# Cutting the last 24 units of a fused attention and MLP kernel into three chunks, two of them with the output's tokens on partitions in a new order

## The chip, the core and the metric

The kernel runs on one core of a Trainium2 chip. The metric is the device time of one execution in microseconds: the median of three runs, 104.57 us for the kernel before (103.97 to 104.58). The profile is of one further execution, which took 104.39 us.

A core has a matrix engine (PE, with its weight loads shown apart as PEld), a vector engine (DVE), an activation engine (ACT), a general engine (POOL) and a queue processor (SP). Here SP issues nearly all DMA transfers. ACT issues a few. Matmuls write into PSUM, from where DVE or ACT carry results to SBUF, and DMA transfers carry them to memory.

## What is computed

A linear attention with a product feature map, for 4 batches, 4 heads, 1088 positions and 32 values per head, and then an MLP over all 4352 tokens:

```python
def phi(x):                       # 8 x 8 = 64 features
    a = np.einsum('rd,bhsd->bhsr', S1, x)
    b = np.einsum('rd,bhsd->bhsr', S2, x)
    return np.einsum('bhsi,bhsj->bhsij', a, b).reshape(*x.shape[:-1], r * r)
q_p, k_p = (phi(q), phi(k))
kv = np.einsum('bhsf,bhsd->bhfd', k_p, v)
z = np.sum(k_p, axis=2)
num = np.einsum('bhsf,bhfd->bhsd', q_p, kv)
den = np.einsum('bhsf,bhf->bhs', q_p, z)[..., None] + 1e-06
attn = num / den
x = attn.transpose(0, 2, 1, 3).reshape(4352, 128)
h = x @ w_in                      # 128 -> 2048
g = h * (1.0 / (1.0 + np.exp(-beta * h)))
out = g @ w_out                   # 2048 -> 128
```

## The kernel before, in words

**Tokens and units.** The 1088 positions of a batch are read as 32 tokens by 34 units: position s is token s // 34, unit s % 34. `xall` (128 x 4352, 2-byte) holds x for all batches, features on partitions and one column per token. Within a batch its columns run unit by unit, 32 tokens each, so column `b * 1088 + u * 32 + t`.

**Attention.** For each batch, steps named by a short code and the batch number make the features, sums and quotients. The last of them is `num`, which writes the batch's x into four strips of PSUM, one for each unit modulo 4: two banks of the tile `xp` and two of `xw`, which takes its place from the same pair of buffers as the MLP's waves. Three copies then bring the strips to `xall`: `xb` (strip 3), `xa` (strip 2), both from `xw`, and `xc` (strips 0 and 1, from `xp`). For the last batch `xb3` runs on ACT, `xa3` and `xc3` on DVE (the function `x_copy`, L579 to L591).

**MLP.** The 136 units of all batches are cut into chunks: eight of 16 units (512 tokens) and a last one of 8 units (256 tokens). A chunk is worked through in waves. A wave fills a PSUM tile of 1024 columns with h for some of the 16 blocks of 128 hidden values (two blocks for 512 tokens, four for 256). This first product is the steps `f<wave>a` and `f<wave>b` (L705, one half of the tile each), with w_in already multiplied by beta, followed by one Silu on ACT into `gT` (L716). The second product, `s<wave>a` and `s<wave>b`, adds that wave's share to the chunk's accumulator (L737): w_out is the weight operand and `gT` streams, so that the result has the 128 output features on partitions and tokens along the row. There are 68 waves: f0 to f63 for the eight large chunks, f64 to f67 for the last.

**Stores.** `o<chunk>` (the function `store`) turns 32 x 32 blocks of a finished accumulator with one DVE transposition into `osb` (L664), and stores it with four transfers per batch that it touches (L670), each for 32 output features: rows of 128 B, 32 tokens as the outermost dimension. The last chunk is different (`store_last`). Its second product has `gT` as the weight operand and w_out streaming (L729), so tokens come out on partitions, two blocks of 128 of them in the two banks of one tile `fin`. Partition p of a block is unit p // 32, token p % 32. ACT copies one bank, DVE the other (L685), and each is stored by one transfer of 128 rows of 512 B, from ACT's queue and from SP's (L686), with the 4 units as the outermost dimension and the 32 tokens inside.

**Order.** Nothing is scheduled automatically. The string `ORDER` lists all steps, and each engine carries out its part in that order. The end of it is: the copies of the last batch around f46 and f47, then chunks 6, 7 and 8, whose second products run some waves behind the first, with o5 and o6 in between, o7 between f67a and f67b, and o8 last.

**PSUM tiles.** `wave` has two buffers. `att2` (two banks: `kpp`, `qpp`, `xp`, at the end `fin`), `acc` (the accumulator of the large chunks) and `att1` (one bank: the small sums of a batch) have one each.

Of the kernel before, what the change touches and what calls it, by code (L numbers as in the profile page):

```python
# [7 lines left out]
F32 = mybir.dt.float32  # L8
F16 = mybir.dt.float16
ALU = mybir.AluOpType  # L10
ACTF = mybir.ActivationFunctionType

P = 128
T = 32
# [3 lines left out]
def kernel(  # L18
# [12 lines left out]
    nc = tc.nc  # L31

    B, H, S, D = q.shape
    R = S1.shape[0]
    F = R * R
    NTOK, DM = out.shape
    DFF = moe_w_in.shape[1]
    NJ = DFF // P
    U = S // T
# [32 lines left out]
    f47a f47b s40b s41a s41b f48a f48b s42a s42b f49a f49b s43a s43b f50a f50b s44a s44b s45a f51a f51b s45b  # L72
    s46a f52a f52b s46b s47a s47b f53a f53b f54a o5 f54b s48a s48b s49a f55a f55b s49b s50a f56a f56b s50b s51a
    f57a f57b s51b s52a s52b f58a f58b s53a s53b f59a f59b s54a s54b s55a s55b f60a f60b f61a o6 f61b s56a s56b
    s57a s57b f62a f62b s58a s58b f63a f63b s59a s59b s60a f64a f64b s60b s61a f65a f65b s61b s62a s62b f66a
    f66b s63a s63b f67a o7 f67b s64a s64b s65a s65b s66a s66b s67a s67b o8
    """

    ENGINES = {
# [12 lines left out]
    ps = ctx.enter_context(tc.tile_pool(name="ps", bufs=1, space=bass.MemoryType.PSUM))  # L92
    ctx.enter_context(tc.manual_schedule())

    def ap(t, offset, dims, p0=0, pn=None):
        pd = list(t.ap[0])
        s = t if pn is None else t[p0 : p0 + pn]
        return bass.AP(tensor=s.tensor, offset=s.offset + offset, ap=[list(s.ap[0])] + dims)

    def ct(shape, dtype, name):  # L100
        return const.tile(shape, dtype, tag=name, name=name)
# [33 lines left out]
    xall = ct([P, B * S], F16, "xall")  # L135

    wave_t = lambda n: ps.tile([P, 2, 512], F32, tag="wave", bufs=2, name=n)
    att2_t = lambda n: ps.tile([P, 2, 512], F32, tag="att2", name=n)
    acc_t = lambda n: ps.tile([P, 512], F32, tag="acc", name=n)

    st = [dict() for _ in range(B)]
# [178 lines left out]
    def eng(name):  # L320
        return {"v": vec, "p": pool}[ENGINES[name]]
# [239 lines left out]
    def num(b, c0, c1):  # L561
# [4 lines left out]
        for f in range(2):  # L566
            for h in range(H):
                for j in range(4):
# [7 lines left out]
                        stop=(f == 1),  # L576
                    )

    def x_copy(b, j, c0, c1, eng):  # L579

        n = min(c1, (U - max(j, 0) + 3) // 4) - c0
        if j < 0:
            eng(
                out=ap(xall, b * S + c0 * P, [[T, 2], [P, n], [1, T]]),
                in_=ap(st[b]["xp", c0][0], 0, [[512, 2], [T, n], [1, T]]),
            )
        else:
            eng(  # L588
                out=ap(xall, b * S + c0 * P + j * T, [[P, n], [1, T]]),
                in_=ap(st[b]["xp", c0][j], 0, [[T, n], [1, T]]),  # L590
            )  # L591


    KC = ((0, 2), (2, 4), (4, 6), (6, 9))
    XPARTS = (("x", (0, 4)), ("", (4, NC)))
    for b in range(B):
# [36 lines left out]
        for x, (c0, c1) in (("", (0, NC)),) if b else XPARTS:  # L633
            step(f"num{x}{b}", num, b, c0, c1)
            for n, j in (("xa", 2), ("xb", 3), ("xc", -1)):
                step(
                    f"{n}{x}{b}",
                    lambda b=b, j=j, c0=c0, c1=c1, k=f"{n}{x}{b}": x_copy(b, j, c0, c1, cop(k)),
                )


    chunks = []
    u = 0
    for n in (16,) * 8 + (8,):
        chunks.append((u, n))
        u += n
    assert u == B * U and chunks[-1][1] == 8
    waves = []
    for ci, (u0, un) in enumerate(chunks):
        per = 1024 // (un * T)  # L650
# [2 lines left out]

    gts, accs, wvs = {}, {}, {}

    LAST = len(chunks) - 1

    def store(ci):
        u0, un = chunks[ci]
        if ci == LAST:  # L660
            store_last(u0, un)
            return
        osb = sb.tile([P, 16, T], F32, tag="osb", bufs=3, name="osb")
        nc.vector.transpose(out=osb[:, :un, :].rearrange("p u m -> p (u m)"), in_=accs[ci][:, : un * T])  # L664
        done = 0
        while done < un:
            b, u = divmod(u0 + done, U)
            n = min(un - done, U - u)
            for m in range(4):
                nc.sync.dma_start(  # L670
                    out=bass.AP(
                        tensor=out.tensor,
                        offset=out.offset + (b * S + u) * DM + m * T,
                        ap=[[U * DM, T], [DM, n], [1, T]],
                    ),
                    in_=osb[T * m : T * m + T, done : done + n, :],
                )
            done += n

    def store_last(u0, un):  # L680

        b, u = divmod(u0, U)
        for i, (copy, e) in enumerate(((nc.scalar.copy, nc.scalar), (nc.vector.tensor_copy, nc.sync))):
            o = ct([P, DM], F32, f"fin_sb{i}")
            copy(out=o, in_=accs[LAST][:, i, 0:DM])  # L685
            e.dma_start(  # L686
                out=bass.AP(
                    tensor=out.tensor,
                    offset=out.offset + (b * S + u + 4 * i) * DM,
                    ap=[[DM, 4], [U * DM, T], [1, DM]],  # L690
                ),
                in_=o,
            )

    def first(s, w):
        ci, n, per, j0 = waves[s]
        u0, un = chunks[ci]
        if s % GP == 0 and w == 0:
            gts[s // GP] = sb.tile([P, GP * 1024], F16, tag="gT", bufs=GB, name="gT")
        if w == 0:  # L700
            wvs[s] = wave_t("wave")
        half, g, o = per // 2, gts[s // GP], s % GP * 1024
        for i in range(half):
            j = j0 + w * half + i
            nc.tensor.matmul(  # L705
                out=wvs[s][:, w, i * n : i * n + n],
                lhsT=winb[:, j * P : j * P + P],
                rhs=xall[:, u0 * T : u0 * T + n],
                start=True,
                stop=True,  # L710
            )
        if s == len(waves) - 1 and w:
            for i in range(2):
                nc.scalar.activation(out=g[:, o + 512 * i : o + 512 * i + 512], in_=wvs[s][:, i], func=ACTF.Silu)
        elif w:
            nc.scalar.activation(  # L716
                out=g[:, o : o + 1024], in_=wvs[s].rearrange("p a n -> p (a n)"), func=ACTF.Silu
            )

    def second(s, w):  # L720
        ci, n, per, j0 = waves[s]
        if j0 == 0 and w == 0:
            accs[ci] = att2_t("fin") if ci == LAST else acc_t("acc")
        half = per // 2
        for i in range(half):
            j, o = j0 + w * half + i, s % GP * 1024 + w * 512 + i * n
            if ci == LAST:
                for a in range(2):
                    nc.tensor.matmul(  # L729
                        out=accs[ci][:, a, 0:DM],  # L730
                        lhsT=gts[s // GP][:, o + a * P : o + a * P + P],
                        rhs=woutp[:, j, :],
                        start=(j == 0),
                        stop=(j == NJ - 1),
                    )
                continue
            nc.tensor.matmul(  # L737
                out=accs[ci][:, :n],
                lhsT=woutp[:, j, :],
                rhs=gts[s // GP][:, o : o + n],  # L740
                start=(j == 0),
                stop=(j == NJ - 1),
            )

    for s in range(len(waves)):
        for w in range(2):
            step(f"f{s}{'ab'[w]}", first, s, w)
            step(f"s{s}{'ab'[w]}", second, s, w)
    for ci in range(len(chunks)):
        step(f"o{ci}", store, ci)  # L750
# [37 lines left out]
```

## Time and profile before

| | |
|---|---|
| median of the runs | 104.57 us (103.97 to 104.58) |
| the profiled execution | 104.39 us |
| its span | 102.6 us, granted clock 0.998 |
| PE busy | 95.2 us (93%), 1294 matmuls |
| ACT busy | 72.3 us (70%) |
| DVE busy | 59.1 us (58%) |
| DMA queue q1 (SP's) | 24756 packets, 12.29 MB, 44.6% of 16 engines |
| chain that ended last | PE 86%, ACT 7%, DVE 1% |
| Silu of 128x1024, L716 | 67 times, mean 1024 ns |
| first product, 128x512 and 128x256, L705 | 144 times, 40.7 us busy |
| second product, 128x512, L737 | 128 times, 36.9 us busy |
| turned second product, 128x128, L729 | 32 times, 1.9 us busy |

The span runs from the first to the last instruction of the program that the profiler saw, so it is shorter than the time of the execution by what lies around it, here 1.8 us. The time column of a matmul counts from its issue to the end of its flow through the array. Matmuls overlap, so the distance between two starts is what one costs in a row of them: 0.43 us for two of 512 columns in the chain. A queue's packets are the pieces that the 16 DMA engines moved, a few bytes of signalling included.

The lines that answer to the places which the change touches stand in the prediction.

### The profile page before, as it was taken

How to read it: one execution, taken by the hardware profiler on the slowest of the kernel's cores; microseconds unless marked ns; L12 is line 12 of the kernel's file. 1: busy time of each engine (PE TensorE's matmuls, PEld its weight loads, DVE VectorE, ACT ScalarE, POOL GpSimd, SP SyncE). 2: the span in 40 equal slices, each digit the busy share in tenths (PEclk: the TensorE clock that was granted, in tenths of full speed). 3: DMA queues.
4: the chain of work that ended last, by engine and by line, in shares of the span. 5: the costliest groups of instructions: out<-in, count | busy, mean ns of one | idle time of the engine just before them, and what ended most of it. 6: DMA issues, size and time to landing. Idle time of an engine off the chain costs nothing.

```text
span 102.6 us, 3065 instructions
## 1 busy us (share of the span) xinstructions
PE 95.2 (93%) x1294; PEld 45.0 (44%) x1294; DVE 59.1 (58%) x107; ACT 72.3 (70%) x92; POOL 40.7 (40%) x49
## 2 busy tenths in 40 slices
PE   5999989999999999999999999999999999999900
PEld 1234554344445454345446433644534444446800
DVE  1564888999798995898953967489240020200210
ACT  1412022687695984789995879999979999899710
POOL 6409689989997993008090000094000000000000
PEclk9999999999999999999999999999999999999999
DMA  2999999986661446613320261051004132022250
GB/s 50 321 255 306 394 378 386 246 270 134 248 217 32 90 127 174 169 27 64 94 70 13 43 114 60 0 101 39 6 13 70 19 52 50 0 44 49 44 101 25
DMA packets 24965, 12.56 MB, mean 122 GB/s; under 512 B 17992, under 2 KB 22648, under 8 KB 24952
## 3 DMA queue, kind: packets, MB, share of 16 engines
q1 hardware_dynamic: 24756, 12.29, 44.6%
q8 instruction: 10, 0.16, 0.7%
q10 hardware_dynamic: 196, 0.08, 0.3%
q14 instruction: 3, 0.02, 0.1%
HBM read 9.84 MB, written 2.23 MB: 118 GB/s over the span
## 4 chain that ended last, share of the span: by engine, by line
PE 86%; ACT 7%; DVE 1%; issue 1%; ACTq 0%
PE wave L705 27%; PE acc L737 24%; PE idle L340 9%; ACT gT L716 6%; PE at L520 6%; PE xp L571 5%; PE qpp L430 3%; PE kpp L357 2%; PE at L450 2%; PE fin L729 2%; PE at L393 2%; PE xw L571 1%; PE at L548 1%; PE at L407 1%; PE cb L393 0%
## 5 line engine op out<-in xcount | busy, mean ns | idle before, releaser
L716 ACT ACTIVATE gT<-wave 128x1024 f16<-128x1024 f32 x67 | 64.8, 1024 | 8.1 <-PE wave L705 7.5
L705 PE MATMUL wave<-xall,winb 128*128 128x512 f16 (+1 forms) x144 | 40.7, 368 | 0.4 <-DVE xall L588 0.2
L737 PE MATMUL acc<-gT,woutp 128*128 128x512 f16 x128 | 36.9, 379 | 0.0
L372 POOL TENSOR_TENSOR qp<-an,tq 128x768 f32<-128x768 f32 (+1 forms) x8 | 14.0, 1760 | 22.1 <-DVE an L496 22.1
L705 PEld LDWEIGHTS <-winb 128*128 128x128 f16 x144 | 13.4, 99 | 17.5 <-issue 3.9
L737 PEld LDWEIGHTS <-woutp 128*128 128x128 f16 x128 | 12.4, 98 | 14.9 <-issue 0.6
L664 DVE STREAM_TRANSPOSE osb<-acc 128x512 f32<-128x512 f32 x8 | 5.7, 714 | 21.1 <-PE acc L737 21.1
L372 POOL TENSOR_TENSOR kp<-tk 128x512 f32<-128x512 f32 (+1 forms) x12 | 15.0, 1276 | 6.4 <-DVE tk L368 6.4
L508 DVE STREAM_TRANSPOSE qpt<-qp 128x768 f32<-128x768 f32 (+1 forms) x13 | 11.1, 883 | 0.3 <-POOL qp L372 0.2
L340 PE MATMUL idle<-warm 128*128 128x512 f16 x30 | 9.6, 454 | 1.3 <-DVE tiny L231 1.3
L344 DVE STREAM_TRANSPOSE kT<-k_in 128x576 f32<-128x576 f32 (+1 forms) x8 | 5.6, 719 | 2.5 <-DMA k_in<-in_k_dram 2.5
L571 PE MATMUL xp<-qpt,kvr 32*32 32x288 f32 (+2 forms) x160 | 6.9, 364 | 0.0
L571 PE MATMUL xw<-qpt,kvr 32*32 32x256 f32 (+1 forms) x160 | 6.8, 343 | 0.0
L349 DVE STREAM_TRANSPOSE qT<-q_in 128x512 f32<-128x512 f32 (+1 forms) x8 | 5.8, 724 | 0.9 <-DMA q_in<-in_q_dram 0.9
L520 PE MATMUL at<-kp,v_in 128*32 128x64 f32 (+1 forms) x288 | 6.3, 223 | 0.0
L520 PEld LDWEIGHTS at<-kp,v_in 128*32 128x32 f32 (+1 forms) x288 | 4.7, 109 | 3.2 <-issue 1.7
L310 POOL TENSOR_TENSOR winb<-w_in_sb,beta_all 128x512 f16<-128x512 f32 x4 | 5.2, 1293 | 0.2 <-DMA beta_all<-in_moe_beta_dram 0.2
L340 PEld LDWEIGHTS <-warm 128*128 128x128 f16 x30 | 2.9, 110 | 4.5 <-issue 1.6
L571 PEld LDWEIGHTS xp<-qpt,kvr 32*32 32x32 f32 x160 | 3.7, 103 | 2.3 <-issue 0.8
L372 DVE TENSOR_TENSOR qp<-an,tq 128x768 f32<-128x768 f32 (+1 forms) x5 | 4.5, 906 | 0.1
L588 ACT CAST xall<-xw 128x128 f16<-128x128 f32 (+1 forms) x8 | 2.4, 325 | 3.0 <-PE xw L571 2.0
L473 DVE TENSOR_TENSOR prod<-tq,tcc 128x288 f32<-128x288 f32 (+2 forms) x5 | 4.1, 818 | 0.1
(75 smaller groups left out, 67.3 us busy)
## 6 DMA issues: line engine op xcount, KB each, us to landing
k_in<-in_k_dram SPq DMA_DIRECT2D x6, 272.0 KB, 5.3
q_in<-in_q_dram SPq DMA_DIRECT2D x6, 272.0 KB, 3.9
out_dram<-osb SPq DMA_DIRECT2D x20, 64.0 KB, 1.9
v_in<-in_v_dram SPq DMA_DIRECT2D x8, 144.0 KB, 4.0
v_in<-in_v_dram SPq DMA_DIRECT2D x8, 128.0 KB, 3.0
w_in_sb<-in_moe_w_in_dram SPq DMA_DIRECT2D x4, 256.0 KB, 4.8
beta_all<-in_moe_beta_dram SPq DMA_DIRECT2D x4, 256.0 KB, 6.9
w_out_sb<-in_moe_w_out_dram SPq DMA_DIRECT2D x4, 256.0 KB, 6.1
```

Source lines behind the costliest of these rows:

```text
L310: eng(name).tensor_tensor(out=winb[:, s], in0=w_in_sb[:, s], in1=beta_all[:, s], op=ALU.mult)
L340: nc.tensor.matmul(out=t[:, 0, :], lhsT=warm[:, 0:P], rhs=warm, start=True, stop=True)
L344: nc.vector.transpose(out=kT[:, u0:u1, :].rearrange("p u t -> p (u t)"), in_=k_in[b][:, u0 * D : u1 * D])
L349: nc.vector.transpose(out=qT[:, u0:u1, :].rearrange("p u t -> p (u t)"), in_=q_in[b][:, u0 * D : u1 * D])
L372: eng.tensor_tensor(out=ap(o, g0 * F, [[F, n], [R, R], [1, R]]), in0=ap(a, g0 * a_step + a_off, [[a_step, n], [1, R], [0, R]]), in1=ap(bsr ...
L508: nc.vector.transpose(out=ap(st[b]["qpt"], c0 * H * F, [[1, (c1 - c0) * H * F]]), in_=ap(st[b]["qp"], c0 * H * F, [[1, (c1 - c0) * H * F]]),)
L520: nc.tensor.matmul(out=t[T * h : T * h + T, :], lhsT=v_in[b][:n, h, c, :], rhs=kp[:n, 4 * c + h, :], start=(done == 0), stop=(done == NC - 1),
L571: nc.tensor.matmul(out=ts[j][T * h : T * h + T, 0 : n * T], lhsT=st[b]["kvr"][p : p + T, f, h, :], rhs=ap(st[b]["qpt"], (4 * c0 + h) * F + ...
L664: nc.vector.transpose(out=osb[:, :un, :].rearrange("p u m -> p (u m)"), in_=accs[ci][:, : un * T])
L705: nc.tensor.matmul(out=wvs[s][:, w, i * n : i * n + n], lhsT=winb[:, j * P : j * P + P], rhs=xall[:, u0 * T : u0 * T + n], start=True, sto ...
L716: nc.scalar.activation(out=g[:, o : o + 1024], in_=wvs[s].rearrange("p a n -> p (a n)"), func=ACTF.Silu)
L737: nc.tensor.matmul(out=accs[ci][:, :n], lhsT=woutp[:, j, :], rhs=gts[s // GP][:, o : o + n], start=(j == 0), stop=(j == NJ - 1),)
```

## The change

The last 24 units, before in chunks of 16 and 8, become three chunks of 8, numbered 7, 8 and 9. Chunks 8 and 9 (the constant `TURNED`, 16 units) both have tokens on partitions. Within each of their blocks of 128 tokens, the order is now token * 4 + unit. Since a block of `gT` columns becomes the weight operand as it lies, this order is set by `xall`: the three copies of the last batch write the last 16 units' columns with a step of 4, and so become two instructions each. `store_last` gives way to `store_turned`, whose transfers have the 32 tokens as the outermost dimension and the 4 units inside. Chunk 8 accumulates in the two banks of `att2` and is copied by DVE and stored from SP's queue. Chunk 9 accumulates in two tiles of one bank, in the places of `acc` and `att1`; one is copied by ACT and stored from its queue, the other by DVE and SP. In `ORDER`, o7 (now of 8 units, still transposed) comes behind s59b, o8 behind s63b, o9 at the end. The number of waves stays at 68.

```diff
-    s57a s57b f62a f62b s58a s58b f63a f63b s59a s59b s60a f64a f64b s60b s61a f65a f65b s61b s62a s62b f66a
-    f66b s63a s63b f67a o7 f67b s64a s64b s65a s65b s66a s66b s67a s67b o8
+    s57a s57b f62a f62b s58a s58b f63a f63b s59a s59b o7 s60a f64a f64b s60b s61a f65a f65b s61b s62a s62b f66a
+    f66b s63a s63b o8 f67a f67b s64a s64b s65a s65b s66a s66b s67a s67b o9
...
+    TURNED = 16
+
     def x_copy(b, j, c0, c1, eng):
 
-        n = min(c1, (U - max(j, 0) + 3) // 4) - c0
-        if j < 0:
+        js, tile = ((0, 1), 0) if j < 0 else ((j,), j)
+        n = min(c1, (U - js[0] + 3) // 4) - c0
+        cut = n
+        if b == B - 1:
+            cut = min(n, (U - TURNED - js[0] + 3) // 4 - c0)
+            assert all((U - TURNED - x + 3) // 4 - c0 == cut for x in js)
+        for k0, k1 in ((0, cut), (cut, n)):
+            if k0 == k1:
+                continue
+            u = 4 * (c0 + k0) + js[0]
+            step_j, step_t = T, 1
+            at = b * S + u * T
+            if k0 == cut and b == B - 1:
+                v = u - (U - TURNED)
+                step_j, step_t = 1, 4
+                at = b * S + (U - TURNED) * T + v // 4 * P + v % 4
+                assert v % 4 + len(js) <= 4
             eng(
-                out=ap(xall, b * S + c0 * P, [[T, 2], [P, n], [1, T]]),
-                in_=ap(st[b]["xp", c0][0], 0, [[512, 2], [T, n], [1, T]]),
+                out=ap(xall, at, [[step_j, len(js)], [P, k1 - k0], [step_t, T]]),
+                in_=ap(st[b]["xp", c0][tile], k0 * T, [[512, len(js)], [T, k1 - k0], [1, T]]),
             )
-        else:
-            eng(
-                out=ap(xall, b * S + c0 * P + j * T, [[P, n], [1, T]]),
-                in_=ap(st[b]["xp", c0][j], 0, [[T, n], [1, T]]),
-            )
...
-    for n in (16,) * 8 + (8,):
+    for n in (16,) * 7 + (8, 8, 8):
...
+    turned = (LAST - 1, LAST)
+
+    def turned_acc(ci):
+        if ci < LAST:
+            t = att2_t("fin")
+            return t[:, 0], t[:, 1]
+        return acc_t("fin0"), ps.tile([P, 512], F32, tag="att1", name="fin1")
 
     def store(ci):
         u0, un = chunks[ci]
-        if ci == LAST:
-            store_last(u0, un)
+        if ci in turned:
+            store_turned(ci)
             return
...
-    def store_last(u0, un):
-
-        b, u = divmod(u0, U)
-        for i, (copy, e) in enumerate(((nc.scalar.copy, nc.scalar), (nc.vector.tensor_copy, nc.sync))):
-            o = ct([P, DM], F32, f"fin_sb{i}")
-            copy(out=o, in_=accs[LAST][:, i, 0:DM])
-            e.dma_start(
+    def store_turned(ci):
+        b, u = divmod(chunks[ci][0], U)
+        for i in range(2):
+            own_queue = ci == LAST and i == 0
+            o = ct([P, DM], F32, f"fin_sb{ci}{i}")
+            (nc.scalar.copy if own_queue else nc.vector.tensor_copy)(out=o, in_=accs[ci][i][:, 0:DM])
+            (nc.scalar if own_queue else nc.sync).dma_start(
                 out=bass.AP(
                     tensor=out.tensor,
                     offset=out.offset + (b * S + u + 4 * i) * DM,
-                    ap=[[DM, 4], [U * DM, T], [1, DM]],
+                    ap=[[U * DM, T], [DM, 4], [1, DM]],
                 ),
                 in_=o,
             )
...
     def second(s, w):
         ci, n, per, j0 = waves[s]
         if j0 == 0 and w == 0:
-            accs[ci] = att2_t("fin") if ci == LAST else acc_t("acc")
+            accs[ci] = turned_acc(ci) if ci in turned else acc_t("acc")
         half = per // 2
         for i in range(half):
             j, o = j0 + w * half + i, s % GP * 1024 + w * 512 + i * n
-            if ci == LAST:
+            if ci in turned:
                 for a in range(2):
                     nc.tensor.matmul(
-                        out=accs[ci][:, a, 0:DM],
+                        out=accs[ci][a][:, 0:DM],
                         lhsT=gts[s // GP][:, o + a * P : o + a * P + P],
```

The Silu call in `first` is written anew so that the last wave's two halves and the other waves share one form; what it issues is the same.

More of the change, by code (lines that the diff above doesn't have):

```diff
@@ L643 @@
     u = 0
-    for n in (16,) * 8 + (8,):
+    for n in (16,) * 7 + (8, 8, 8):
         chunks.append((u, n))
         u += n
-    assert u == B * U and chunks[-1][1] == 8
+    assert u == B * U and TURNED == sum(n for _, n in chunks[-2:])
     waves = []
@@ L711, in first @@
             )
[L712 to L715, printed above, removed]
+        m = 2 if s == len(waves) - 1 else 1
+        for i in range(m if w else 0):
             nc.scalar.activation(
-                out=g[:, o : o + 1024], in_=wvs[s].rearrange("p a n -> p (a n)"), func=ACTF.Silu
+                out=g[:, o + i * 512 : o + i * 512 + 1024 // m],
+                in_=wvs[s].rearrange("p a n -> p (a n)")[:, i * 512 : i * 512 + 1024 // m],
+                func=ACTF.Silu,
             )
```

## The prediction

> **What bounds the kernel now.** I read the page first. Its rows in 40 slices show PE at 8 or 9 tenths from the second slice to the 38th, and two empty slices after that. So there are two places to price: the stretch in which PE runs without a gap, and the tail behind its last matmul. The page's chain, asked for the last 8 us, shows how they meet:
>
> ```profile
> 94.84 0.43 PE acc L737 x2
> 95.27 0.44 PE wave L705 x4
> 95.71 1.80 PE fin L729 x32
> 97.51 0.02 issue
> 97.53 0.28 ACT fin_sb L685
> 97.81 0.02 issue
> 97.83 0.29 DVE fin_sb L685
> ```
>
> Columns are start, length, what. The second product of the last chunk ends at 97.51, and then two copies of one size run one behind the other: DVE starts when ACT is done, though it reads another bank. In the timeline the two final stores are issued at 97.83 (ACT's queue, 0.65) and 98.15 (SP's, 0.70). The span ends at 102.6, so the tail behind PE is 5.1 us, of which the copies are 0.6. What fills the rest I read from the windows (PE, PEld, DVE, ACT, POOL busy, granted clock, DMA share, GB/s) and from the DMA view for 99.05 us to the end:
>
> ```profile
> 98.50:99.00 0.50, 0.00 (x0) 0.00 (x0) 0.00 (x0) 0.00 (x0) 0.00 (x0) 1.00 0.77 131
> 99.00:99.50 0.50, 0.00 (x0) 0.00 (x0) 0.00 (x0) 0.00 (x0) 0.00 (x0) 1.00 0.17 43
> 99.50:100.00 0.50, 0.00 (x0) 0.00 (x0) 0.00 (x0) 0.00 (x0) 0.00 (x0) 1.00 0.28 81
> 100.00:100.50 0.50, 0.00 (x0) 0.00 (x0) 0.00 (x0) 0.00 (x0) 0.00 (x0) 1.00 0.28 78
> 100.50:101.00 0.50, 0.00 (x0) 0.00 (x0) 0.00 (x0) 0.00 (x0) 0.00 (x0) 1.00 0.20 60
> 101.00:101.50 0.50, 0.00 (x0) 0.00 (x0) 0.00 (x0) 0.00 (x0) 0.00 (x0) 1.00 0.00 0
> ```
>
> ```profile
> q10 hardware_dynamic: 132, 0.07, 6.2%
> q1 hardware_dynamic: 132, 0.07, 5.7%
> ```
>
> Until 99.0 the engines are three quarters busy with the four `osb` stores of chunk 7, issued from 96.05. From 99.1 to 101.0 they move the two `fin_sb` stores at a share of only 0.28, about 4 of 16 engines. The packet counts say the same: each store has 128 rows of 512 B, and 132 packets are 128 and 4 more, one per engine that took part. Both have an outermost dimension of 4. The `osb` stores, outermost dimension 32, reach a share of 1.05 in a quarter of a microsecond. After the last packet there are 1.6 us of landing and closing that the change does not touch.
>
> The Trainium skill, page "DMA: Bandwidth & Descriptors", section "Why a DMA increments its semaphore by 16 and not by 1", has this as a rule: a store runs on the largest number of engines, 16 at most, that divides the slowest dimension of both patterns. By it the old final stores get 4 engines and the new ones 16; the trace agrees with the 4 (132 packets, share 0.28).
>
> The other place is the copies of the last batch's x:
>
> ```profile
> 75.00 0.37 ACT L588 CAST xall<-xw 128x256 f16<-128x256 f32 x1 [0.72 <-PE xw L571]
> 75.40 0.42 DVE L588 CAST xall<-xw 128x256 f16<-128x256 f32 x1 [1.22 <-ACT xall L588]
> 75.75 0.75 DVE L583 CAST xall<-xp 128x576 f16<-128x576 f32 x1
> 75.88 0.59 PE L705 MATMUL wave<-xall,winb 128*128 128x512 f16 x2 [0.20 <-DVE xall L588]
> ```
>
> xb3 on ACT, then xa3 on DVE, then PE's f47, which had idled 0.20 for xa3. These two copies are on the path; xc3 (DVE, 75.75 to 76.50) is not, because its first reader is f48 at 76.96.
>
> **The change, part by part.** Sums are for the profiled execution, 104.39 us (span 102.6 and 1.8 outside it); the median of the three runs is 104.57, so 0.18 above it.
>
> *Copies in two pieces.* Each of xb3, xa3, xc3 becomes a copy of the units up to 17 and one of the last 16, the second written with a step of four 2-byte elements. In the built order DVE's first piece waits for both ACT pieces, so nothing overlaps. ACT: two copies of 128x128 in a row took 0.44 (at 17.31), against 0.37 for the one of 128x256, so +0.07. DVE: 128 columns took 0.29 and 256 took 0.42 (L685, L588), and the next DVE copy started 0.08 before the end of the one ahead (75.75 against 75.83); two pieces are 0.29 + 0.29 - 0.08 = 0.50, +0.08. Together +0.15 before f47. xc3 as 320 and 256 columns grows by about as much and ends near 76.8; its first piece, which f48 needs, is done by 76.5, so that costs nothing; without that cover it would be 0.1. No row shows a 2-byte write with a step. Below, I see no way for two copies to be shorter than one, so 0 is the floor, with f47's later work absorbing it; above, I allow twice the cost per written column, 128 x (0.8 + 1.04) ns = +0.24 more, so 0.4. I take 0.15, nearest to the rows that have this size.
>
> The Trainium skill, page "SBUF — State Buffer", section "Door 1: The DMA port swizzle", says that accesses with two hits per 16-byte line run at full rate; a step of 8 bytes has just two, so by it the step is free. No run here shows it.
>
> *Chunk 7 cut in two.* The number of waves stays 68, and so do ACT's Silu calls of 1024 columns. On PE the eight waves f56 to f63 have four matmuls of 256 for two of 512: 0.44 against 0.43 in the chain, +0.01 each. Chunk 7's second product goes from 512 to 256 columns, again 0.44 for 0.43 per wave, x4. Chunk 8's is turned around: 32 matmuls of 128 columns, 1.80 as in the `fin` row, against 16 of 512 over half the waves, 4 x 0.43 = 1.72, +0.08. Sum 0.08 + 0.04 + 0.08 = 0.2. PE has no gap from 89.5 to 97.5 (8.00 busy of 8.00), so most of it counts; before that ACT, 0.92 a wave, hides some. I take 0.13, with 0 and 0.2 as ends.
>
> *Stores moved.* o7 (four stores of half the size) moves ahead by four waves; its transposition needs DVE, idle then. o8 is new: two DVE copies and two SP stores behind s63b, near 95.3, where o7's transposition was. On SP's queue eight issues of o6 run from 89.46 to 94.43; o7's four at about 0.5 end near 96.4, o8's two at up to 0.70 with gaps near 97.9. The last SP store is ready at about 98.1, so the queue is clear by 0.2; if not, what is over goes straight to the end. The data of o7 and o8 are gone before the last stores begin.
>
> *The tail.* `fin0` and `fin1` are now separate tiles, and in the built order DVE waits for PE alone: the copies run side by side, SP's issue comes 0.30 sooner. The two stores spread over 16 engines. The 264 packets took 11.9% of 16 engines over 3.59 us, 6.8 engine-us: 1.7 us on 4 engines, 0.43 on 16. From issue to first packet, the `osb` store issued at 96.05 took 0.83 (first packets in the slice at 96.88); ACT's `fin_sb` store took 1.27 (97.83 to 99.1), partly behind the `osb` packets that filled all engines. I take the middle, 1.05, and keep both ends.
>
> **The sum.** PE ends at 97.51 + 0.15 + 0.13 = 97.79; DVE's copy with its issue gaps at 98.11; SP issues at 98.13; first packets 99.18; last 99.61, for 101.0 before: -1.4. 104.39 - 1.4 = 103.0. Lower end: PE +0, first packet 0.83, which gives 97.51 + 0.34 + 0.83 + 0.43 = 99.1, -1.9, 102.5. Upper end: copies 0.4, PE 0.2, first packet 1.27: 100.15, -0.85, 103.5. 0.70.
>
> **The rivals.**
> - *SP's last issue held up* (0.14). One of o6's issues took 1.64 where its like take 0.46, at 91.28, and the DMA view of 91 to 93 us has one packet on the instruction queue (q8, 0.02 MB) in that place. The change gives PE 96 more loads and matmuls, so another fetch may fall on the last SP stores. Price 1.64 - 0.46 = 1.18: last issue 99.31, last packet about 100.6, so -0.4: 104.0. Against: ten such fetches served 2600 PE instructions, and the tenth comes at 91 us; 96 more need not bring an eleventh.
> - *The spread does not follow* (0.05): still 4 engines, for some reason that a store of this form, which the trace has not, would show. Then 0.30 is won and 0.28 lost: 104.4, no change.
> - *Slower: the stepped write is dear* (0.07). It is the one operation with no row. Each multiple of the plain cost per column, 128 x (0.8 + 1.04) = 0.24 us, delays f47 and all behind it. The 1.4 are eaten at six times more, sevenfold cost; at twelvefold it is 11 x 0.24 - 1.4 = +1.2: 105.6. For: 32 columns no longer lie side by side. Against: the same engines read and write patterns of two and three dimensions at the plain rate elsewhere (L583: 0.75 for 576 in runs of 32).
> - *Slower: weight loads come to light* (0.04). Chunk 8 loads `gT` as weights between other loads; a load takes 98 ns. If each of the 32 stood alone, 32 x 0.098 = +3.1: 106.1. Against: the 32 of `fin` ran at 56 ns apiece with the same loads hidden.
>
> **Numbers.** One per cent, 1.05 us, is about what a measurement of this kernel can tell from no change. Of the forecast's 0.70, 0.64 lie below 103.5; the first rival adds 0.03 there. Faster 0.67. Same: 0.06, 0.11 of the first rival, 0.04 of the second, 0.02 of the third: 0.23. Slower: 0.05, 0.04 and 0.01: 0.10. The range, from just under the lower end to the first rival's time, 102.4 to 104.1, leaves out about 2 in 10; the likeliest case alone has 102.5 to 103.5.
>
> **What would show it.** In the profile after: each final store with 128 + 16 packets on its queue and a DMA share near 0.8 or more for half a microsecond; DVE's last copy waiting for PE; last packet near 99.6; f47 at about 76.0; PE's last matmul at about 97.8. Wrong would be: a share that stays near 0.3; an SP issue of over a microsecond behind 95 us; a copy of 128 columns above 0.35; weight loads that make chunk 8's second product longer than 2 us.

## The result and the profile after

The changed kernel takes 103.5 us in the median of 21 runs (103.0 to 106.65), the kernel before, in runs beside it, 104.46. The ratio is 0.9921, with a 95% interval of 0.9893 to 0.995: 0.8% faster. Ratios and intervals here and below leave disturbed executions out. The profiled execution took 103.39 us against 104.39, with a span of 101.6 against 102.6.

The tail is the first thing to look at. First the chain of the last 8 us of the changed kernel (start, length, what), then the windows behind it (PE, PEld, DVE, ACT, POOL busy, granted clock, DMA share, GB/s), then the packets of the two queues from 99.05 us on:

```profile
94.96 0.11 PE wave L725
95.07 0.45 PE fin L749 x8
95.52 0.44 PE wave L725 x4
95.95 1.80 PE fin L749 x32
97.75 0.02 issue
97.78 0.29 DVE fin_sb L705
```

```profile
98.50:99.00 0.50, 0.00 (x0) 0.00 (x0) 0.00 (x0) 0.00 (x0) 0.00 (x0) 1.00 0.00 0
99.00:99.50 0.50, 0.00 (x0) 0.00 (x0) 0.00 (x0) 0.00 (x0) 0.00 (x0) 1.00 0.35 102
99.50:100.00 0.50, 0.00 (x0) 0.00 (x0) 0.00 (x0) 0.00 (x0) 0.00 (x0) 1.00 0.56 160
```

```profile
q1 hardware_dynamic: 144, 0.07, 7.9%
q10 hardware_dynamic: 144, 0.07, 7.9%
```

One copy of 0.29 us is left in the chain where there were two. Each store has 144 packets, 128 rows and 16 more, where it had 132: 16 engines take part. The packets are through within 0.65 us instead of 1.9. But from 98.5 to 99.0 the DMA engines do nothing at all, though both stores are issued at 98.02 and 98.09. And PE ends 0.24 later than before, at 97.75 for 97.51.

Why PE ends later is seen in the copies of the last batch's x (timeline: start, length, what, and in brackets the idle time ahead of it and what ended that):

```profile
74.59 0.61 ACT L601 CAST xall<-xw 128x128 f16<-128x128 f32 x2 [0.72 <-PE xw L571]
75.23 0.64 DVE L601 CAST xall<-xw 128x128 f16<-128x128 f32 x2 [1.46 <-ACT xall L601]
75.68 1.14 DVE L601 CAST xall<-xp 128x320 f16<-128x320 f32 x2
76.02 0.59 PE L725 MATMUL wave<-xall,winb 128*128 128x512 f16 x2 [0.75 <-DVE xall L601]
```

ACT's copies take 0.61 instead of 0.37, DVE's 0.64 instead of 0.42, and PE waits 0.75 for them instead of 0.20. The start of these copies, 74.59 against 75.00, has nothing to do with the change: everything ahead of it is the same in both kernels, and over the 14 profiles of this study it lies between 74.45 and 75.59. For the experiments I therefore take the span apart at four points: the start of the first of these copies, the start of f47's matmuls, the end of PE's last matmul in the chain, and the end of the last data packet.

| us | copies to f47 | f47 to PE's end | PE's end to last packet | to the span's end | sum |
|---|---|---|---|---|---|
| before | 0.88 | 21.63 | 3.48 | 1.65 | 27.64 |
| after | 1.43 | 21.73 | 2.17 | 1.73 | 27.06 |

The changed part of the execution is 0.58 us shorter; the remaining 0.4 of the 1.0 us between the two profiles lies ahead of it. The medians give 0.96, and the interval of the ratio 0.5 to 1.1.

### The profile page after: what moved, and what is told of

Its sections match the earlier page's. It is cut to its first block, busy times and chain, and to the rows that moved or that the text cites. A ratio compares the mean times of both kernels' runs of the same rounds, so it can differ in the third digit from the quotient of the medians.

```text
span 101.6 us, 3172 instructions
## 1 busy us (share of the span) xinstructions
PE 94.9 (93%) x1342; PEld 48.2 (47%) x1342; DVE 59.3 (58%) x111; ACT 72.5 (71%) x93; POOL 40.6 (40%) x49
## 4 chain that ended last, share of the span: by engine, by line
PE 86%; ACT 8%; DVE 1%; issue 1%; DVEq 0%; ACTq 0%
PE wave L725 27%; PE acc L757 23%; PE idle L340 9%; ACT gT L734 7%; PE at L520 6%; PE xp L571 5%; PE fin L749 4%; PE qpp L430 3%; PE at L450 2%; PE kpp L357 2%; PE at L393 2%; PE xw L571 1%; PE at L548 1%; ACT xall L601 1%; PE at L407 1%
## 5 line engine op out<-in xcount | busy, mean ns | idle before, releaser
L734 ACT ACTIVATE gT<-wave 128x1024 f16<-128x1024 f32 (+1 forms) x69 | 65.8, 1011 | 8.3 <-PE wave L725 7.8
L757 PE MATMUL acc<-gT,woutp 128*128 128x512 f16 (+1 forms) x128 | 34.7, 366 | 0.0
L725 PEld LDWEIGHTS <-winb 128*128 128x128 f16 x160 | 14.7, 99 | 16.7 <-issue 3.8
L684 DVE STREAM_TRANSPOSE osb<-acc 128x512 f32<-128x512 f32 (+1 forms) x8 | 5.4, 680 | 18.0 <-PE acc L757 15.1
L749 PE MATMUL fin<-woutp,gT 128*128 128x128 f16 x64 | 4.4, 219 | 0.0
```

The source lines that it names most:

```text
L725: nc.tensor.matmul(out=wvs[s][:, w, i * n : i * n + n], lhsT=winb[:, j * P : j * P + P], rhs=xall[:, u0 * T : u0 * T + n], start=True, sto ...
L734: nc.scalar.activation(out=g[:, o + i * 512 : o + i * 512 + 1024 // m], in_=wvs[s].rearrange("p a n -> p (a n)")[:, i * 512 : i * 512 + 10 ...
L749: nc.tensor.matmul(out=accs[ci][a][:, 0:DM], lhsT=gts[s // GP][:, o + a * P : o + a * P + P], rhs=woutp[:, j, :], start=(j == 0), stop=(j ...
L757: nc.tensor.matmul(out=accs[ci][:, :n], lhsT=woutp[:, j, :], rhs=gts[s // GP][:, o : o + n], start=(j == 0), stop=(j == NJ - 1),)
```

## The experiments

Twelve more kernels ran, 6 to 12 times each. The table has the same four parts for each, in the same order ("PE" is f47 to PE's end, "closing" the stretch from the last packet to the span's end), and its ratio to the kernel before in runs beside it.

| | copies | PE | tail | closing | sum | ratio, 95% interval |
|---|---|---|---|---|---|---|
| e1 plain step | 1.10 | 21.73 | 2.18 | 1.72 | 26.73 | 0.9896 (0.9861 to 0.9931) |
| e2 plain, 4 engines | 1.10 | 21.73 | 3.44 | 1.71 | 27.98 | 1.0028 (1.0005 to 1.005) |
| e3 one piece | 0.88 | 21.73 | 2.18 | 1.73 | 26.52 | 0.9944 (0.9914 to 0.9975) |
| e4 last chunk only | 1.27 | 22.16 | 2.22 | 1.64 | 27.29 | 0.9962 (0.9933 to 0.9991) |
| e5 xw by DVE | 1.11 | 21.75 | 2.17 | 1.74 | 26.77 | 0.993 (0.9888 to 0.9972) |
| e6 pairs | 0.82 | 21.74 | 2.17 | 1.71 | 26.44 | 0.992 (0.9892 to 0.9948) |
| e7 one store | 1.12 | 21.74 | 2.15 | 1.65 | 26.66 | 0.9931 (0.9893 to 0.9968) |
| e8 before, two tiles | 0.88 | 22.16 | 3.42 | 1.64 | 28.10 | 1.008 (1.005 to 1.011) |
| e9 the same, other places | 0.88 | 21.64 | 3.37 | 1.65 | 27.54 | 0.9985 (0.9954 to 1.0017) |
| e10 last chunk only, other places | 1.27 | 21.63 | 2.24 | 1.64 | 26.78 | 0.9925 (0.9894 to 0.9956) |
| e11 the same with pairs | 0.82 | 21.64 | 2.25 | 1.64 | 26.35 | 0.9858 (0.9825 to 0.9891) |
| e12 four small stores | 0.88 | 21.63 | 3.42 | 1.81 | 27.74 | 1.0015 (0.9986 to 1.0043) |

**e1 and e3: what the copies cost.** e1 takes the step out of the second pieces (so it leaves the turned order out of `xall`, as e2 and e3 do, and only its time is of use):

```diff
-                step_j, step_t = 1, 4
-                at = b * S + (U - TURNED) * T + v // 4 * P + v % 4
+                pass
```

> The changed kernel with its copies still in two pieces, but the second piece written without the step of 4, so columns of the last 16 units lie as before and the rows of chunks 8 and 9 go out permuted. Measured from the end of num (74.97 before, 74.57 after) f47 started 0.91 us later before and 1.45 later after. Theory A, the stepped write is what costs: 1.05 to 1.15 here, time 0.3 to 0.4 us under the changed kernel's. Theory B, the second instruction and its waits cost: about 1.4 here, time as the changed kernel's. Both: last packet 2.2 us after PE's last matmul.

e3 does not cut the copies at all:

```diff
-        if b == B - 1:
+        if False:
             cut = min(n, (U - TURNED - js[0] + 3) // 4 - c0)
...
-            if k0 == cut and b == B - 1:
+            if False:
```

> The changed kernel with the three copies of the last batch in one piece each, without a step, as in the kernel before (rows of chunks 8 and 9 go out permuted). Theory A: f47 0.9 us after the end of num, so 0.5 to 0.55 sooner than in the changed kernel, and time down by as much; this is what the whole order of columns costs. If less than 0.3 of it arrives at the end, PE and ACT take it up on the way.

Of the 0.55 us by which f47 starts later, 0.33 go with the step (e1: 1.10) and 0.22 with the second instruction (e1 against e3: 1.10, 0.88). The 0.22 has two parts. The copies themselves take 0.12 longer (0.95 in e1, 0.83 in e3, from the start of the first to the end of the last one that f47 needs). The other 0.09 lies between that end and f47's start: 0.15 us in the five kernels in which ACT and DVE both copy `xw` in two pieces (the changed one, e1, e2, e4, e10), 0.05 to 0.06 in the nine others. Why is not shown. In the changed kernel's groups by shape, two copies of the same size stand side by side, the stepped one of the last batch and a plain one of an earlier batch (busy, mean ns):

```profile
L601 DVE CAST xall<-xp 128x256 f16<-128x256 f32 x1 | 0.7, 709 | 0.0
...
L601 DVE CAST xall<-xw 128x256 f16<-128x256 f32 x1 | 0.4, 425 | 1.1 <-ACT xall L601 1.1
```

e1's last copy of that form:

```profile
L600 DVE CAST xall<-xp 128x256 f16<-128x256 f32 x1 | 0.4, 415 | 0.0
```

A step of four 2-byte elements costs DVE (709 - 415) / 256 = 1.15 ns per column on top of about 1 ((0.42 - 0.29) / 128). So theory A is right for the larger share and theory B for the smaller. The traces give e3 0.54 less than the changed kernel, but its ratio doesn't show that: 0.9944, where the sums would give about 0.989. Its profiled execution took 102.68 us, the shortest of its eight runs; the next is 103.34. Why the ratio is that high stays open. I go by the traces for the copies, because that part repeats: it is 0.88 in all five kernels that copy as before, 1.10 in e1 and e2, and 1.27 in e4 and e10.

**e2: the spread.** As e1, with the stores as the old last chunk had them:

```diff
-                    ap=[[U * DM, T], [DM, 4], [1, DM]],
+                    ap=[[DM, 4], [U * DM, T], [1, DM]],
```

> As the run before, and the four stores of chunks 8 and 9 with the 4 units outermost and the 32 tokens inside, as the old last chunk had them. From PE's last matmul to the last packet it took 3.48 us before and 2.17 after. Theory A, the gain is the spread over 16 engines: 64 packets per engine instead of 16 at 27 ns, +1.3, so 3.4 to 3.5 here, and time 1.2 to 1.3 us over the run before. Theory C, the gain is that chunk 7's stores are out of the way and the copies run side by side: 2.2 to 2.7 here.

The tail grows from 2.18 to 3.44, that is by 1.26, and the ratio from 0.9896 to 1.0028, 1.3%. e2's windows look like those of before:

```profile
99.50:100.00 0.50, 0.00 (x0) 0.00 (x0) 0.00 (x0) 0.00 (x0) 0.00 (x0) 1.00 0.26 72
100.00:100.50 0.50, 0.00 (x0) 0.00 (x0) 0.00 (x0) 0.00 (x0) 0.00 (x0) 1.00 0.28 74
100.50:101.00 0.50, 0.00 (x0) 0.00 (x0) 0.00 (x0) 0.00 (x0) 0.00 (x0) 1.00 0.28 86
```

Everything of the change but the step and the spread is in e2, and it is no faster than the kernel before. The order of the two outer dimensions of a store is the whole gain. Theory C falls.

**e8 and e9: the copies side by side alone.** In the kernel before, the last chunk's halves get two tiles:

```diff
...
-            accs[ci] = att2_t("fin") if ci == LAST else acc_t("acc")
+            accs[ci] = (acc_t("fin0"), ps.tile([P, 512], F32, tag="att1", name="fin1")) if ci == LAST else acc_t("acc")
...
```

> The kernel before with the last chunk's two halves in two separate tiles, so that DVE's last copy does not wait for ACT's; nothing else is changed. The copy comes 0.30 us sooner. Theory A, the stores are limited by 4 engines and by chunk 7's packets ahead of them: the last packet is at most 0.1 sooner, time within 0.1 of the kernel before. Rival: the issue is the limit, and 0.3 arrives at the end.

It came out slower, by 0.8%, which neither theory had. The tail was as in theory A (3.42), but PE's stretch grew by 0.53. e8's chain shows why:

```profile
95.02 0.73 DVE osb L664
95.75 0.04 issue
95.79 1.96 PE fin L729 x32
97.75 0.02 issue
97.78 0.29 DVE fin_sb L685
```

`fin0` sits in the one buffer of `acc`, and there chunk 7's transposition is still reading. PE, which in the kernel before has no gap here, waits for DVE. e9 takes `att2_t("fin0")[:, 0]` instead of `acc_t("fin0")`.

> As e8, with the two halves in the places of att2 and att1, so that the last second product does not wait for chunk 7's accumulator: in e8 it stood 0.37 us behind chunk 7's transposition, and from f47 to PE's end it took 22.15 against 21.61. Expected 21.6 again. From PE's end to the last packet 3.43 in e8 against 3.50 before: if the copies side by side are worth 0.05 to 0.1 here too, the time is within 0.15 of the kernel before; if they are worth their 0.3, it is 0.3 under it.

PE's stretch is 21.64 again and the time that of the kernel before. The tail is 3.37 against 3.48: copies side by side are worth 0.1, not 0.3. One reason is on SP's queue (start, length):

```profile
96.74 1.04 SPq L670 DMA_DIRECT2D out_dram<-osb  x2
97.88 0.69 SPq L686 DMA_DIRECT2D out_dram<-fin_sb  x1
```

DVE's copy is done at 97.62, but SP still issues chunk 7's last store.

**e4 and e10: the last chunk alone.** Chunks and `ORDER` as before, and of the change only this for the chunk of 8:

```diff
...
-    TURNED = 16
+    TURNED = 8
...
-    for n in (16,) * 7 + (8, 8, 8):
+    for n in (16,) * 8 + (8,):
...
-    turned = (LAST - 1, LAST)
+    turned = (LAST,)
```

> Chunks as before (eight of 16 units, one of 8), only the last one with tokens as token * 4 + unit, stored on 16 engines from separate tiles; o7 as before between f67a and f67b. Theory A, the spread is the gain: the last two stores wait for chunk 7's packets, which end about 1.5 us behind PE's last matmul, then 0.45 us: last packet 2.0 to 2.2 behind PE, as in the changed kernel, and the time the same or up to 0.3 lower, because half as many columns are stepped. Theory C, clearing chunk 7 out of the way is the gain: last packet 2.7 to 3.2 behind PE, time 0.5 to 1.0 above the changed kernel's.

The tail is 2.22, as theory A had it, though chunk 7's packets run until 99.30, 0.58 us before the first packet of the last stores. But PE's stretch is 22.16, for the reason of e8: `fin` waits 0.37 us for DVE's transposition of chunk 7. In the changed kernel, o7 comes early enough to free `acc`; here it does not. e10 has `fin0` in `att2`.

> As e4, with the halves in the places of att2 and att1. From the end of num: copies 1.34 as in e4, PE 21.6 to 21.7 where e4 had 22.15, to the last packet 2.2, to the span's end 1.65: 26.8 together, against 27.1 for the changed kernel and 27.7 before. Time 0.2 to 0.4 under the changed kernel's, so cutting chunk 7 in two brings nothing by itself. If the cut matters otherwise, the tail is longer than 2.5 or PE's stretch longer than 21.9.

21.63 and 2.24, and a sum of 26.78 against 27.06 for the changed kernel; the ratios are alike (0.9925 and 0.9921). So cutting chunk 7 in two, with the second half turned as well, brings nothing by itself. It lengthens PE's stretch by 0.10 and the copies by 0.16, and its one use is to free `acc` for `fin0`, which another place for `fin0` makes needless.

**e5 and e6: cheaper copies.** e5 gives DVE both strips of `xw`:

```diff
+        if b == B - 1 and j == 3:
+            return
         js, tile = ((0, 1), 0) if j < 0 else ((j,), j)
+        if b == B - 1 and j == 2:
+            js, tile = (2, 3), 2
```

> The changed kernel with both strips of xw (xb3 and xa3) copied by DVE in two instructions, plain and stepped, and nothing by ACT. If the wait of DVE for ACT is what makes the two copies add up, one engine without the hand-over is no slower: f47 1.05 to 1.15 us after the end of num (0.42 plain + 0.6 to 0.65 stepped) against 1.45, time 0.2 to 0.4 below the changed kernel. If the stepped write costs more on DVE than on ACT, 1.3 or more, and no gain.

1.11 against 1.43, as expected, and the stepped copy of 256 columns still takes 0.71. e6, on top of e5, writes the same columns in another order, two neighbours and then the step:

```diff
...
+            if step_t == 4:
+                eng(
+                    out=ap(xall, at, [[P, k1 - k0], [4, T], [1, 2]]),
+                    in_=ap(st[b]["xp", c0][tile], k0 * T, [[T, k1 - k0], [1, T], [512, 2]]),
+                )
+                continue
```

> As the run before, with the stepped copies of two strips written in another order: for each token the two neighbouring columns first (4 bytes side by side), then the step to the next token. If a step costs per jump to a new place, half as many jumps: the stepped copy of 256 columns falls from about 0.7 to about 0.55 us. If reading from two banks in turn costs, it is above 0.7.

```profile
L606 DVE CAST xall<-xw 128x256 f16<-128x256 f32 x1 | 0.4, 416 | 0.0
L606 DVE CAST xall<-xp 128x256 f16<-128x256 f32 x1 | 0.4, 415 | 0.0
```

These are e6's two stepped copies: 416 and 415 ns, as fast as a plain one, better than the 0.55 that was expected. Reading from two banks in turn costs nothing. f47 starts 0.82 behind the first copy, sooner than in the kernel before. The two ratios, 0.993 and 0.992, are too close to tell e5, e6 and the changed kernel apart; the traces do.

**e7: one store.** As e5, with the columns ordered so that each partition holds two rows of the output that are neighbours in memory. The stores of chunks 8 and 9 become

```diff
...
+            copy(out=o[:, i * DM : i * DM + DM], in_=accs[ci][i][:, 0:DM])
+        nc.sync.dma_start(
...
+                ap=[[U * DM, T], [2 * DM, 4], [1, 2 * DM]],
```

> As e5, with the columns in an order that puts two units of a token side by side in a partition, so that chunks 8 and 9 go out in one store each, 128 rows of 1024 B from SP's queue. After the change SP's last store is issued at 98.10 and its first packet comes 1.2 us later, ACT's 0.3 after that. Theory: the queues are served one after the other, so one store saves the second: last packet 1.75 to 1.95 us behind PE's last matmul against 2.17, time 0.2 to 0.4 under e5. Rival: the delay to the first packet is what counts and does not shrink, 1.2 us and 0.4 to 0.5 for the packets: 2.0 to 2.2, no gain.

The tail is 2.15, so the rival holds: one store is issued at 98.83, its first packet runs at 100.08, 1.25 us later, and the last ends 0.52 after that.

**e12: 16 engines without turning.** Each half of e9's last chunk leaves in four stores:

```diff
...
+            for m in range(4):
+                e.dma_start(
...
+                        ap=[[U * DM, T], [1, DM]],
...
+                    in_=o[T * m : T * m + T, :],
```

> As e9, and each half of the last chunk goes out in four stores of 32 partitions (32 rows of 512 B), four from ACT's queue and four from SP's, so that 16 engines take part without any turning of columns. An osb store, which also reads 32 partitions, has its first packet 0.83 us behind its issue, the stores of 128 partitions 1.2 to 1.3. If that delay goes by the form, the last issue comes 1.4 to 1.6 us behind the first and the last packet 2.6 to 2.8 behind PE's end: 27.0 from the end of num, as the changed kernel. If the eight issues hold each other up on the two queues, 3.2 or more and no gain on the kernel before.

The delay to the first packet does go by the form in part: 0.94 us for ACT's first small store against 1.29 for its store of 128 rows in e11. But the issues use that up, four on each queue:

```profile
98.09 2.12 SPq L687 DMA_DIRECT2D out_dram<-fin_sb  x4
```

The tail is 3.42 and the time that of the kernel before. So what the turned columns buy is few issues.

**e11: the version that beats both.** e10 with the copies of e6.

> As e10, with both strips of xw copied by DVE, and in the stepped pieces the two neighbouring columns of a token first, as in e6, where a stepped copy of 256 columns took 0.416 against 0.71. From the end of num: copies 0.85 to 0.95, PE 21.6 to 21.7, tail 2.2, end 1.65: 26.3 to 26.5, 1.2 to 1.4 under the kernel before and 0.6 to 0.8 under the changed one. A rival: ACT, freed from its copy, brings Silu forward and PE's stretch shortens too, up to 0.2 more.

```profile
74.64 0.56 DVE L611 CAST xall<-xw 128x384 f16<-128x384 f32 x1 [0.82 <-PE xw L571]
75.12 0.28 DVE L606 CAST xall<-xw 128x128 f16<-128x128 f32 x1
75.31 0.61 DVE L611 CAST xall<-xp 128x448 f16<-128x448 f32 x1
75.46 0.60 PE L735 MATMUL wave<-xall,winb 128*128 128x512 f16 x2
```

102.85 us against 104.21, a ratio of 0.9858 (0.9825 to 0.9891; the changed kernel's is 0.9893 to 0.995). The sum is 26.35, 1.29 under the kernel before and 0.71 under the changed one, which agrees with the expected parts. PE's stretch is no shorter, so the rival of this run falls.

## Why the prediction was right, and where its sizes were off

The forecast was 103.0 us in a range of 102.4 to 104.1, by 1.4 less in the profiled execution; it came to 103.5, and to 0.8% less. So the time lies in the range, but at 103.5, where the forecast's own sum had its upper end, and the gain is 0.96 us in the medians and 0.58 in the parts of the two traces, not 1.4. The mechanism was right: a share of 0.28 and 132 packets read as 4 of 16 engines, and e2 shows that undoing the spread alone gives the whole gain back. The Trainium skill's rule in "DMA: Bandwidth & Descriptors", section "Why a DMA increments its semaphore by 16 and not by 1", fits all of it: 16 engines with 32 outermost (144 packets), 4 with 4 (132).

- *Copies in two pieces*: +0.15 forecast, between 0 and 0.4; 0.55 measured (1.43 - 0.88), above that upper end. This is the term that was most mis-sized. The second instruction cost 0.22, the step 0.33. I had put the step at nothing because no row showed one, and bounded it by twice the plain cost per column. It costs rather more than that: 1.15 ns more on 1.0 for DVE, and for ACT (450 - 271) / 128 = 1.4 ns more on 0.8. The copies in two pieces without a step were 0.12 longer, near the 0.15; the 0.09 between the last copy and f47 had no term. The Trainium skill's rule quoted from "SBUF — State Buffer", section "Door 1: The DMA port swizzle", by which the step would be free, does not hold for these writes: 709 ns against 415.
- *Chunk 7 cut in two*: +0.13 forecast, 0.10 measured (21.73 - 21.63).
- *Stores moved*: nothing forecast. SP's queue was clear in time: its next to last store was issued at 96.70, and the last did not wait for it. e10 shows that the move was not needed.
- *The tail*: from PE's end to the last packet 1.82 forecast, 2.17 measured, for 3.48 before. Its three terms were 0.34 to SP's issue, 1.05 from there to the first packet and 0.43 for the packets; they came to 0.34, 1.20 (98.09 to 99.29) and 0.63. So two terms were too small.
  - The delay was taken as the middle of 0.83 and 1.27, because I had put part of the 1.27 down to chunk 7's packets ahead of it. In e8 those packets had ended 0.6 us before the first one of ACT's store, and its delay was 1.29 all the same; in e7, long after them, it was 1.25. So it belongs to this form of store, and the row of the same form was the one to take. (In the changed kernel ACT's store, issued first, ran behind SP's: 1.55, from 98.02 to 99.57.)
  - The packets' engine time was worked out over 3.59 us, but the view runs from 99.05 to 103, which is 3.95: 11.9% of 16 engines over that is 7.5 engine-us, so 1.9 on 4 engines and 0.47 on 16. After the change it is 7.2 (15.8% over the 2.85 us of that view), and 0.63 us for it means 0.7 of 16 engines, not all. That the engine time hardly changed also speaks against the rival that a packet had become cheaper in the new order of rows: more engines share the same work. The forecast of the spread, 1.7 - 0.43 = 1.27, agrees with e2's 1.26 because both sizes were about 0.2 too small.
  - The copies side by side count for 0.1 (e9), where the second rival had set down 0.30. SP's issue did come 0.30 sooner (0.34 behind PE's end for 0.64), but in the kernel before ACT's store, issued 0.32 behind PE's end, had its packets first.
- *The sum*: 0.55 + 0.10 - 1.31 + 0.08 in the closing = -0.58 in the traces, for -1.4.
- *The signs*: f47 at 76.02 and PE's end at 97.75 are as forecast (76.0 and 97.8), but by luck: the copies started 0.41 earlier than in the profile before, and from there to PE's end 0.65 was lost, not 0.28. The DMA share came to 0.7 for 0.63 us instead of 0.8 for half a microsecond. One of the signs of being wrong did show: stepped copies of 128 columns took 0.45 (ACT) and 0.43 (DVE), above 0.35.
- *The rivals*: no issue on SP took over a microsecond in the tail, and chunk 8's weight loads stayed hidden (1.80 for 32 in the chain, 0.45 for 8). The stepped write was dear, as the third rival had it, but by its own measure (0.24 us for each multiple of the plain cost) 0.33 makes it between two- and threefold; it would have had to be sevenfold to eat the gain.

## What to carry to other kernels

When the last transfers run at a flat, low DMA share, compare it with the outermost dimension of their patterns, and count the packets beyond the data: a dimension of 4 there left 12 of 16 engines idle, and exchanging two dimensions was worth 1.3% of this kernel. The new order has to be paid for somewhere; here a copy that wrote 2-byte elements one by one with a step was the price, and writing two neighbours at a time took it away. And when a tile is split to free one engine from another, look at what the new tile's buffer last held: in e8 that wait cost more than the split brought.

## What was not expected

- A stepped write of single 2-byte elements took 709 ns for 256 columns on DVE, the same columns in neighbouring pairs 415. On ACT, 128 columns with a step took 450 ns, without one 271. Whether it is the pair of 4 bytes or the order of the two dimensions that matters was not taken further apart.
- The first packet of a store of 128 partitions ran 1.2 to 1.3 us behind its issue, also where the DMA engines were idle meanwhile, of an `osb` store of 32 partitions 0.83 to 0.84, and of the two such stores in the changed kernel SP's ran first and ACT's behind it (99.29 and 99.57), though ACT's had been issued first.
- The part ahead of the last batch's copies is the same in all fourteen profiled kernels, and it ended between 74.45 and 75.59. That is more than most of the effects here. Parts measured between two events of one trace resolved what medians of 6 to 12 runs could not.
